# A cached-attention decode kernel: the scheduling context's critical section spans the whole program instead of the first loads alone

## The chip, the cores and the metric

The kernel runs on one core of one Trainium2 chip. The metric is the device time of one execution in microseconds (us); the figure that is compared is the median of several executions. Five runs of the kernel before gave a median of 666.26 us, with a lowest of 666.04 and a highest of 666.57. Beside the times there is one profiled execution, which took 666.55 us.

The core has five engines that run their own instruction streams: PE (TensorE, matrix products), DVE (VectorE), ACT (ScalarE), POOL (GpSimd) and SP (SyncE). They are ordered only by semaphores. SP and ACT each issue DMAs on a queue of their own, and all DMAs run on the same 16 DMA engines.

## The reference

One decoding step of a pre-norm transformer block, for four sequences and one new position each. The attention reads a cache of 4096 positions for 32 heads of 128, so that the keys and the values are 134 MB each and nearly all of the input. Cut to what matters:

```python
# x: (4, 1, 640); k_cache, v_cache: (4, 32, 4096, 128); all bfloat16
def _A_ref(x, k_cache, v_cache, wq, wo):
    q = (x @ wq).reshape(4, 1, 32, 128).transpose(0, 2, 1, 3)
    scores = jnp.einsum("bhqd,bhkd->bhqk", q, k_cache) * 128 ** -0.5
    p = softmax(scores)
    o = jnp.einsum("bhqk,bhkd->bhqd", p, v_cache)
    return o.transpose(0, 2, 1, 3).reshape(4, 1, 4096) @ wo

def _B_ref(x, w1, b1, w2):                       # 640 -> 1728 -> 640
    h = x @ w1 + b1
    return (h * jnp.tanh(softplus(h))) @ w2

h = x + _A_ref(layernorm(x), k_cache, v_cache, wq, wo)
out = h + _B_ref(layernorm(h), w1, b1, w2)
```

## The kernel before

**Tiling.** The 32 heads are taken in four groups of eight, and each group is worked through for the four sequences: 16 steps `i`, with `hg, b = divmod(i, 4)`. In a step the keys of eight heads of one sequence lie in one SBUF slot, 128 partitions x 32768 bfloat16 (8.4 MB): 16 partitions for each head, 256 positions on each partition. The values lie in another slot in the same way. There are three such slots, A, B and C. Keys go to A, B, A, B (`KS`) and values to C, C, A, C (`VS`). DVE multiplies the keys in place by the query (`mult`, L503), PE adds groups of products by matmuls with the identity (`fold`, L705), DVE finishes the sums (`reduce`, L514), ACT takes the exponential, and PE multiplies by the values (`pv_mm`). The normalisation of a group of heads runs at the head of the next group's turn (`norm`, `heads`). PE's work for the four groups is one hardware loop of four turns (`Fori`, L917). After the last turn `pe_tail` does the output projection, the second layer norm and the dense block.

**Order and queues.** Nothing is left to a scheduler: each engine's program is written out by hand as a Python function (`sync_prog`, `pool_prog`, `act_prog`, `dve_prog`, `pe_prog`), and each is in the order in which it is issued. `Prog.do` emits an instruction and counts up a semaphore; `Prog.need` emits a wait for a count. The functions run twice: once dry, to note at which count each event happens, and once live. SP issues every large load: `wq` (5.2 MB, into slot C), the first two key blocks, then values and keys in turn as the slots come free, and at last the weights `wo`, `w1` and `w2`. ACT issues the small loads of `x` and of the bias `b1`. Each of them stores one half of the output (`store`, L248), on semaphores `OUT0` and `OUT1`.

**Head.** The program is built inside a tile context of the language. `first_loads` (L275) holds the loads of `wq`, `x`, key block 0 and key block 1. It is emitted alone inside a critical section of that context (L936 and L937), and then the context is closed (`tc.close()`, L939). The critical section and the closing emit instructions of their own, on the lines L936 and L939 of the profile: SP counts up a semaphore when its part of the section ends, the engines that took part answer by one each and SP waits for these answers; then come a barrier of all five engines, a clear of the context's own three semaphores by POOL, and a second such barrier. A barrier is a DRAIN on each engine that counts up one semaphore, a wait for the count of four by POOL, an increment by POOL of a release semaphore, and a wait for that on each of the other engines. Only after the second barrier do the five hand-written programs begin (L941 and L942). They allocate their semaphores straight from the core (`nc.alloc_semaphore`, L118), so that the context does not clear them.

**Tail.** After its half of the store, SP, and ACT after its half, calls `leave` (L254): it counts up `FIN`, waits until its own half has landed (`OUT0` or `OUT1` at 16) and takes the 16 off again. POOL, which has nothing to do by then, runs `clear` (L260): it waits for `FIN` at 2 and clears the other 24 semaphores in two ranges. Those instructions are on L257, L258, L262 and L263. After them each engine's program simply ends.

Of the kernel before, what the change touches and what calls it, by code (L numbers as in the profile page):

```python
# [72 lines left out]
def kernel(  # L73
# [13 lines left out]
    nc = tc.nc  # L87

    N, _, D = A_x.shape
    _, H, Sk, Dh = A_k_cache.shape  # L90
    F = B_w1.shape[1]
    P = 128
    DC = D // P
# [18 lines left out]
    SCALE = float(Dh) ** -0.5  # L112
    EPS = 1e-5

    book = Book()
    WSEM = ["WQ", "WT"] + [f"W{k}" for k in range(9)]
    for s in ["PE", "DV", "DVP", "DVA", "AC", "ACP", "PO", "KA", "KB", "VA", "VC", "X", "S", "OUT0", "OUT1", "FIN"] + WSEM:
        book.handles[s] = nc.alloc_semaphore(s)  # L118

    SB0, SLOT0 = 16512, 229344 - 3 * SLOT * 2  # L120
    at = [SB0]
# [1 line left out]
    def sb(name, shape, dt, region=at, top=SLOT0):  # L123
        size = 4 if dt == FP32 else 2
        for d in shape[1:]:
            size *= d
        size = -(-size // 32) * 32
        t = nc.alloc_sbuf_tensor_at(name, shape, dt, offset=region[0]).ap()
        region[0] += size
        assert region[0] <= top, (name, region[0])  # L130
        return t

    slot = {
        c: nc.alloc_sbuf_tensor_at(f"slot{c}", (P, SLOT), BF16, offset=SLOT0 + k * SLOT * 2).ap()
        for k, c in enumerate("ABC")
    }
# [28 lines left out]
    wq = slot["C"][:, 0 : DC * H * Dh].rearrange("p (c n) -> p c n", c=DC)  # L165
    x_bf = sb("x_bf", (N, D), BF16, setup, topC)
# [57 lines left out]
    x_rows = A_x.rearrange("b s d -> (b s) d")  # L224
# [5 lines left out]
    KS = {0: "A", 1: "B", 2: "A", 3: "B"}  # L230
    VS = {0: "C", 1: "C", 2: "A", 3: "C"}

    sp = Prog(nc.sync, book)
    po = Prog(nc.gpsimd, book)
    ac = Prog(nc.scalar, book)
# [3 lines left out]
    def tiles(src, i):  # L239
        hg, b = divmod(i, N)  # L240
        return src[b, hg * G : (hg + 1) * G].rearrange("h (q r) d -> (h q) (r d)", q=PG)

    def load(p, dst, src, key, sem):
        p.do(lambda: p.eng.dma_start(out=dst, in_=src), key, sem, 16)

    def store(p, h):
        c, n = CG // 2, D // 2
        p.need("o_bf")  # L248
        load(
            p, out_rows[:, h * n : (h + 1) * n].rearrange("b (k o) -> k b o", k=c),  # L250
            o_bf[h * P // 2 : (h + 1) * P // 2 : ROW, :], ("out", h), f"OUT{h}",
        )

    def leave(p, h):  # L254
        fin, o = book.handles["FIN"], book.handles[f"OUT{h}"]
        if p.live:
            p.eng.sem_inc(fin, 1)  # L257
            p.eng.wait_ge(o, 16).then_inc(o, -16)  # L258

    def clear():  # L260
        fin = book.handles["FIN"]
        nc.gpsimd.wait_ge(fin, 2).then_inc(fin, -2)  # L262
        nc.clear_and_free_semaphores(  # L263
            [h for k, h in book.handles.items() if k not in ("OUT0", "OUT1", "FIN")]
        )

    def k_load(i):
        c = KS[i % N]
        load(sp, slot[c][:, :], tiles(A_k_cache, i), ("K", i), "K" + c)

    def v_load(i):
        c = VS[i % N]
        load(sp, slot[c][:, :], tiles(A_v_cache, i), ("V", i), "V" + c)

    def first_loads():  # L275
        load(
            sp, slot["C"][:, 0 : DC * H * Dh], A_wq.rearrange("(p c) n -> p (c n)", c=DC), "wq", "WQ"
        )
        load(ac, x_bf[:, :], x_rows[:, :], "x", "X")
        k_load(0)  # L280
        k_load(1)

    def sync_prog():
        for hg in range(NHG):
            i = hg * N
            if hg:
                sp.need(("PV", i - 2))
                k_load(i)
                sp.need(("F", i - 1, NS - 1))
                k_load(i + 1)  # L290
            sp.need(("PV", i - 1) if hg else ("qb", NHG - 1))
            v_load(i)
            sp.need(("F", i, NS - 1))
            k_load(i + 2)
            sp.need(("PV", i))
            v_load(i + 1)
            sp.need(("F", i + 1, NS - 1))
            k_load(i + 3)
            sp.need(("F", i + 2, NS - 1))
            v_load(i + 2)  # L300
            sp.need(("PV", i + 1))
            v_load(i + 3)
        sp.need(("F", NT - 1, NS - 1))
        for q in range(NHG):
            load(
                sp, wo_sb[:, q, :, :],
                A_wo[q * QN : (q + 1) * QN, :].rearrange("(p j) n -> p j n", j=G), ("wo", q), f"W{q}",
            )
        w1_v = B_w1.rearrange("(p c) n -> p c n", c=DC)
        for k, (c0, c1) in enumerate(zip(W1S, W1S[1:])):  # L310
            load(sp, w1_sb[:, c0:c1, :], w1_v[:, c0:c1, :], ("w1", c0), f"W{NHG + k}")
        sp.need(("PV", NT - 2))
        load(sp, w2_tail[0:FT, :], B_w2[FM * P : F, :], "w2t", "WT")
        w2_v = B_w2[0 : FM * P, :].rearrange("(p j) n -> p j n", j=FM)
        for k, (j0, j1) in enumerate(zip(W2S, W2S[1:])):
            load(sp, w2_sb[:, j0:j1, :], w2_v[:, j0:j1, :], ("w2", j0), f"W{NHG + 2 + k}")
        store(sp, 0)
        leave(sp, 0)

    def pool_prog():  # L320
        g = nc.gpsimd
# [19 lines left out]

    def act_prog():
        a = nc.scalar
        ac.need("b1z")
        load(ac, b1T[:, 0:FM], B_b1[0 : FM * P].rearrange("(p j) -> p j", j=FM), "b1a", "S")
        load(ac, b1T[0:FT, FM : FM + 1], B_b1[FM * P : F].rearrange("(p o) -> p o", o=1), "b1b", "S")
        ac.need("eps", "mv")
        ac.do(
            lambda: a.activation(
                out=std[:, :], in_=mv[:, 1:2], func=ACT.Sqrt, bias=eps[0:N, :], scale=1.0  # L350
            ),
            "std", "AC",
        )
        for h in range(2):
            ac.need(("q", h))
            ac.do(
                lambda: a.copy(out=q_all[:, h * 512 : (h + 1) * 512], in_=red[:, h, :]),
                ("qa", h), "ACP",
            )
        for hg in range(NHG):  # L360
            ac.need(("qb", hg))
            ac.do(
                lambda: a.copy(
                    out=q_bc[:, hg, :, :].rearrange("p b d -> p (b d)"), in_=red[:, (2 + hg) % 4, :]
                ),
                ("qc", hg), "AC",
            )

        ac.need("ident")
        ac.do(  # L370
            lambda: a.copy(
                out=pv_sb[:, :, :], in_=ident[:, :].unsqueeze(1).to_broadcast([P, RQ, Dh])
            ),
            ("pvc", -1), "ACP",
        )

        def exp(i, s):
            b = i % N
            sl = slice(s * RS, (s + 1) * RS)
            ac.need(("R", i, s))  # L380
            ac.do(
                lambda: a.activation(  # L382
                    out=ex[:, sl], in_=s_f[:, sl], func=ACT.Exp, scale=SCALE,
                    accum_out=rs[:, b, s : s + 1],
                ),
                ("exp", i, s), "AC",
            )

        def copy(i):
            ac.need(("PV", i))  # L390
            ac.do(
                lambda: a.copy(  # L392
                    out=pv_sb[:, :, :].rearrange("p r d -> p (r d)"), in_=pv[:, :]
                ),
                ("pvc", i), "ACP",
            )

        for i in range(NT):
            b = i % N
            if i and b == 0:  # L400
                copy(i - 1)
            for s in range(NS):
                exp(i, s)
                if (b, s) in ((1, 1), (2, 2), (3, 2)):
                    copy(i - 1)
        copy(NT - 1)
        ac.need("var")
        ac.do(
            lambda: a.activation(
                out=std2[:, :], in_=var[:, :], func=ACT.Sqrt, bias=eps[:, :], scale=1.0  # L410
            ),
            "std2", "AC",
        )
        ac.need("h1")
        ac.do(
            lambda: a.activation(out=ta[:, :, :], in_=h1[:, :, :], func=ACT.Exp, scale=1.0),  # L416
            "ta", "AC",
        )
        store(ac, 1)
        leave(ac, 1)  # L420

    def dve_prog():
        v = nc.vector
# [485 lines left out]
    def pe_prog(live):  # L909
# [16 lines left out]

    progs = (
        (sp, sync_prog), (po, pool_prog), (ac, act_prog), (dv, dve_prog), (pe, lambda: pe_prog(pe.live))
    )
    first_loads()  # L930
    for p, f in progs:
        f()
    book.ready = True
    for p, f in progs:
        p.restart(True)
    with tc.tile_critical(name="k", no_gpsimd_drain=True):  # L936
        first_loads()  # L937
    tc.close()
    tc.compile()  # L939
    for p, f in progs:  # L940
        f()  # L941
        if p is po:  # L942
            clear()


# [28 lines left out]
```

The softmax here doesn't subtract the row's maximum and nothing guards it: scores larger than these inputs give would overflow.

## Time and profile before

| what | value |
|---|---|
| median of 5 runs | 666.26 us (666.04 to 666.57) |
| the profiled execution, its own time | 666.55 us |
| its span, first to last instruction | 665.1 us |
| what lies around the span | 1.45 us |
| bytes read from HBM | 283.35 MB, 426 GB/s over the span |
| DMA queue of SP, share of 16 engines | 98.9% |
| busy DVE, PE, ACT, POOL | 407.3, 399.3, 41.6, 3.3 us |

In the page's strip of 40 slices a digit is the busy share of a slice in tenths. In a timeline each line has the start, the time taken, the engine, the line of the kernel, the operation, what is written and what is read; `q` after an engine's name stands for its instruction queue, where DMAs are issued and semaphores are waited for. A question about one line of the kernel answers with the operations on it, how often each ran, the shortest, the median and the longest duration in ns, and the first and the last start in us. The wait of an instruction is not part of its duration: its start is the moment when its wait ended.

### The profile page before, as it was taken

What the parts mean: (1) busy time and instruction counts of PE and PEld (TensorE: products, weight loads), DVE (VectorE), ACT (ScalarE), POOL (GpSimd) and SP (SyncE); (2) the same over time, 40 slices, a digit from 0 to 9 for tenths busy, and PEclk for the clock granted to TensorE, in tenths of its full rate; (3) what the DMA queues carried; (4) which work ended last, traced back from release to release, by engine and by line L of the source; (5) the groups of instructions that cost most, each with busy time, mean ns of one, the idle gap of its engine ahead of it and who ended that gap; (6) DMA issues with size and microseconds to landing.
All of it is one profiled execution on the core that took longest, in us unless ns stands there. A gap on an engine that the chain in (4) does not pass through costs nothing. (4 is left out here: it accounts for less than half of the span.)

```text
span 665.1 us, 5193 instructions
## 1 busy us (share of the span) xinstructions
PE 399.3 (60%) x2747; PEld 80.2 (12%) x1787; DVE 407.3 (61%) x252; ACT 41.6 (6%) x158; POOL 3.3 (0%) x15
## 2 busy tenths in 40 slices
PE   0856658668317595848408395838335666755767
PEld 0600000101101010101100010100010001010147
DVE  1077988486048778677218798759207688948602
ACT  0200000000000000000000000000000000000011
POOL 1000000000000000000000000000000000000000
PEclk9768787968659796868658887879776769887865
DMA  9999999999999999999999999999999999999996
GB/s 379 439 438 441 415 414 441 439 434 439 431 438 426 426 441 422 441 434 441 438 418 434 441 422 441 434 438 442 410 441 434 426 441 438 438 430 422 438 401 250
DMA packets 6390, 283.50 MB, mean 426 GB/s; under 512 B 936, under 2 KB 1004, under 8 KB 1516
## 3 DMA queue, kind: packets, MB, share of 16 engines
q1 hardware_dynamic: 6138, 283.35, 98.9%
q8 instruction: 7, 0.11, 0.1%
q10 hardware_dynamic: 242, 0.01, 0.0%
q14 instruction: 3, 0.02, 0.0%
HBM read 283.35 MB, written 0.01 MB: 426 GB/s over the span
## 5 line engine op out<-in xcount | busy, mean ns | idle before, releaser
L503 DVE TENSOR_TENSOR slotA<-slotA,q_bc 128x8192 bf16<-128x8192 bf16 x32 | 140.7, 4416 | 106.3 <-DMA slotA<-in_A_k_cache_dram 106.3
L503 DVE TENSOR_TENSOR slotB<-slotB,q_bc 128x8192 bf16<-128x8192 bf16 x32 | 140.7, 4418 | 15.9 <-DMA slotB<-in_A_k_cache_dram 15.9
L514 DVE TENSOR_REDUCE s_f<-red 128x64 f32<-128x1024 f32 x64 | 78.0, 1219 | 101.7 <-PE red L705 101.6
L705 PE MATMUL red<-slotA,ident 128*128 128x512 bf16 x480 | 138.2, 452 | 0.0
L705 PE MATMUL red<-slotB,ident 128*128 128x512 bf16 x480 | 129.6, 430 | 0.0
L695 PE MATMUL red<-slotA,ident 128*128 128x512 bf16 x32 | 14.2, 445 | 120.1 <-PEq L49 120.1
L695 PE MATMUL pv<-slotC,e 128*32 128x512 bf16 x768 | 52.7, 436 | 37.9 <-PEq L49 37.9
L695 PE MATMUL red<-slotB,ident 128*128 128x512 bf16 x32 | 14.2, 443 | 86.6 <-PEq L49 86.6
L382 ACT ACTIVATE ex<-s_f 128x64 bf16<-128x64 f32 x64 | 16.4, 256 | 505.9 <-DVE s_f L514 505.9
L528 DVE TENSOR_TENSOR e<-ex,hmask 128x512 bf16<-128x512 bf16 x64 | 39.8, 684 | 0.0
L695 PEld LDWEIGHTS pv<-slotC,e 128*32 128x32 bf16 x768 | 22.7, 108 | 96.6 <-issue 83.2
L695 PEld LDWEIGHTS red<-slotA,ident 128*128 128x128 bf16 x32 | 3.2, 99 | 189.1 <-issue 189.0
L695 PEld LDWEIGHTS red<-slotB,ident 128*128 128x128 bf16 x32 | 3.2, 99 | 170.9 <-issue 170.9
L695 PEld LDWEIGHTS o_ps<-pv_sb,selo 128*32 128x32 f32 x136 | 13.5, 109 | 64.0 <-issue 63.9
L695 PE MATMUL o_ps<-pv_sb,selo 128*32 128x128 f32 x136 | 18.0, 276 | 0.0
L695 PE MATMUL pv<-slotA,e 128*32 128x512 bf16 x256 | 14.5, 380 | 0.6 <-PEq L49 0.6
L392 ACT COPY pv_sb<-pv 128x512 f32<-128x512 f32 x16 | 9.4, 586 | 72.3 <-PE pv L695 72.3
L382 ACT ACTIVATION_READ_ACCUMULATOR ex<-s_f 128x1 f32 x64 | 11.9, 186 | 0.0
L695 PE MATMUL red<-q_all,sel 32*128 32x128 bf16 x128 | 10.0, 269 | 0.8 <-PEq L49 0.8
L695 PEld LDWEIGHTS red<-q_all,sel 32*128 32x128 bf16 x128 | 9.8, 122 | 1.7 <-issue 1.7
L695 PEld LDWEIGHTS pv<-slotA,e 128*32 128x32 bf16 x256 | 6.7, 97 | 25.3 <-issue 19.5
L553 DVE RECIPROCAL rl<-misc 32x1 f32<-32x1 f32 x4 | 0.6, 150 | 14.8 <-PE misc L695 14.8
(95 smaller groups left out, 78.0 us busy)
## 6 DMA issues: line engine op xcount, KB each, us to landing
slotC<-in_A_wq_dram SPq DMA_DIRECT2D x1, 5120.0 KB, 15.5
slotB<-in_A_wo_dram SPq DMA_DIRECT2D x4, 1280.0 KB, 16.8
slotB<-in_B_w_dram SPq DMA_DIRECT2D x1, 1296.0 KB, 23.5
slotA<-in_B_w_dram SPq DMA_DIRECT2D x1, 960.0 KB, 27.3
slotB<-in_B_w_dram SPq DMA_DIRECT2D x1, 864.0 KB, 25.8
slotA<-in_B_w_dram SPq DMA_DIRECT2D x1, 800.0 KB, 28.7
slotA<-in_B_w_dram SPq DMA_DIRECT2D x1, 320.0 KB, 29.0
slotC<-in_A_v_cache_dram SPq DMA_DIRECT2D x12, 45.1
```

What stands on the lines that cost most here:

```text
L382: lambda: a.activation(out=ex[:, sl], in_=s_f[:, sl], func=ACT.Exp, scale=SCALE, accum_out=rs[:, b, s : s + 1],),
L392: lambda: a.copy(out=pv_sb[:, :, :].rearrange("p r d -> p (r d)"), in_=pv[:, :]),
L503: lambda: v.tensor_tensor(out=t, in0=t, in1=q_bc[:, hg, b, :].unsqueeze(1).to_broadcast([P, RS, Dh]), op=ALU.mult,),
L514: lambda: v.tensor_reduce(out=s_f[:, s * RS : (s + 1) * RS], in_=red[:, k : k + 2, :].rearrange("p k (r c) -> p (k r) c", c=CW), axis=AX.X ...
L528: lambda: v.tensor_tensor(out=e[:, sl, :], in0=ex[:, sl].unsqueeze(2).to_broadcast([P, RS, G]), in1=hmask[:, :].unsqueeze(1).to_broadcast( ...
L553: dv.do(lambda: v.reciprocal(out=rl[:, :], in_=l_ps), ("rl", hg), DV)
L695: lambda: nc.tensor.matmul(out_, lhsT=lhsT, rhs=rhs, start=start, stop=stop, skip_group_check=skip),
L705: return t.add_instruction(mybir.InstMatmult(name=nc.get_next_instruction_name(), engine=mybir.EngineType.PE, ins=[t.lower_ap(rhs), t.lowe ...
```

## The change

The critical section is entered at the top of the kernel function and is left when the function returns, so that all five programs stand inside it. The closing of the context, with its answers, barriers and clear, comes behind everything else. The semaphores are allocated from the context, which clears them there; `FIN`, `leave` and `clear` go away. The first loads are at the head of `sync_prog` and `act_prog`. At its end SP waits for both halves of the output; ACT waits for neither.

In the built programs the instructions between the first loads and the output stores are the same, in the same order on each engine, with the same waits, in both kernels. What stands elsewhere is this:

- Ahead of the programs: PE, DVE and POOL wait by a branch for the section to open, as SP and ACT do in both kernels. The three steps that stood between the first loads and the programs (answers, first barrier, clear, second barrier) are gone from there.
- Behind the programs, on SP: a wait for `OUT1`, a branch that waits for `OUT0`, the count-up that ends the section, SP's own answer, two waits and a NOP that waits, for the answers of all five engines, and the two barriers.
- Behind the programs, on ACT, PE, DVE and POOL: the answer (which waits for SP's count-up) and the two barriers.
- Between the two barriers POOL clears one range of 32 semaphores: the 26 of the kernel and six of the context.

```diff
+    ctx.enter_context(tc.tile_critical(name="k", no_gpsimd_drain=True))
+
     book = Book()
     WSEM = ["WQ", "WT"] + [f"W{k}" for k in range(9)]
-    for s in ["PE", "DV", "DVP", "DVA", "AC", "ACP", "PO", "KA", "KB", "VA", "VC", "X", "S", "OUT0", "OUT1", "FIN"] + WSEM:
-        book.handles[s] = nc.alloc_semaphore(s)
+    for s in ["PE", "DV", "DVP", "DVA", "AC", "ACP", "PO", "KA", "KB", "VA", "VC", "X", "S", "OUT0", "OUT1"] + WSEM:
+        book.handles[s] = tc.alloc_semaphore(s)
...
-    def leave(p, h):
-        fin, o = book.handles["FIN"], book.handles[f"OUT{h}"]
-        if p.live:
-            p.eng.sem_inc(fin, 1)
-            p.eng.wait_ge(o, 16).then_inc(o, -16)
-
-    def clear():
-        fin = book.handles["FIN"]
-        nc.gpsimd.wait_ge(fin, 2).then_inc(fin, -2)
-        nc.clear_and_free_semaphores(
-            [h for k, h in book.handles.items() if k not in ("OUT0", "OUT1", "FIN")]
-        )
...
-    def first_loads():
-        load(
-            sp, slot["C"][:, 0 : DC * H * Dh], A_wq.rearrange("(p c) n -> p (c n)", c=DC), "wq", "WQ"
-        )
-        load(ac, x_bf[:, :], x_rows[:, :], "x", "X")
-        k_load(0)
-        k_load(1)
+    def sync_prog():
+        load(sp, slot["C"][:, 0 : DC * H * Dh], A_wq.rearrange("(p c) n -> p (c n)", c=DC), "wq", "WQ")
...
         for hg in range(NHG):
             i = hg * N
             if hg:
                 sp.need(("PV", i - 2))
-                k_load(i)
+            k_load(i)
+            if hg:
                 sp.need(("F", i - 1, NS - 1))
-                k_load(i + 1)
+            k_load(i + 1)
...
         store(sp, 0)
-        leave(sp, 0)
+        sp.need(("out", 0), ("out", 1))
...
     def act_prog():
         a = nc.scalar
+        load(ac, x_bf[:, :], x_rows[:, :], "x", "X")
...
         store(ac, 1)
-        leave(ac, 1)
...
-    first_loads()
     for p, f in progs:
         f()
     book.ready = True
     for p, f in progs:
         p.restart(True)
-    with tc.tile_critical(name="k", no_gpsimd_drain=True):
-        first_loads()
-    tc.close()
-    tc.compile()
-    for p, f in progs:
         f()
-        if p is po:
-            clear()
```

More of the change, by code (lines that the diff above doesn't have):

```diff
@@ L252, in store, with k_load, v_load @@
         )
-    def leave(p, h):
-        fin, o = book.handles["FIN"], book.handles[f"OUT{h}"]
-        if p.live:
-            p.eng.sem_inc(fin, 1)
-            p.eng.wait_ge(o, 16).then_inc(o, -16)
-    def clear():
-        fin = book.handles["FIN"]
-        nc.gpsimd.wait_ge(fin, 2).then_inc(fin, -2)
-        nc.clear_and_free_semaphores(
-            [h for k, h in book.handles.items() if k not in ("OUT0", "OUT1", "FIN")]
-        )
[L267 to L273, printed above, removed]
-    def first_loads():
-        load(
-            sp, slot["C"][:, 0 : DC * H * Dh], A_wq.rearrange("(p c) n -> p (c n)", c=DC), "wq", "WQ"
-        )
-        load(ac, x_bf[:, :], x_rows[:, :], "x", "X")
-        k_load(0)
-        k_load(1)
-    def sync_prog():
+    def sync_prog():
+        load(sp, slot["C"][:, 0 : DC * H * Dh], A_wq.rearrange("(p c) n -> p (c n)", c=DC), "wq", "WQ")
+        def k_load(i):
+            s = KS[i % N]
+            load(sp, slot[s][:, :], tiles(A_k_cache, i), ("K", i), "K" + s)
+        def v_load(i):
+            s = VS[i % N]
+            load(sp, slot[s][:, :], tiles(A_v_cache, i), ("V", i), "V" + s)
         for hg in range(NHG):
```

## The prediction

> **What bounds the kernel now.** I read the page's strip and its DMA queues first, then the timeline of the first 17 us and of the last 3 us, and last the single lines on which the context's own instructions stand. The strip and the queues say what the 665.1 us are made of:
>
> ```profile
> DMA  9999999999999999999999999999999999999996
> GB/s 379 439 438 441 415 414 441 439 434 439 431 438 426 426 441 422 441 434 441 438 418 434 441 422 441 434 438 442 410 441 434 426 441 438 438 430 422 438 401 250
> q1 hardware_dynamic: 6138, 283.35, 98.9%
> HBM read 283.35 MB, written 0.01 MB: 426 GB/s over the span
> ```
>
> The 16 DMA engines are busy in every slice, and only the last falls off. So 283 MB of cache and weights bound the kernel, and an edit can act in two places: ahead of the first load or behind the last one. The change lies in just these two places, so the timeline is read there. This is the head:
>
> ```profile
> 0.97 0.38 SPq L244 DMA_DIRECT2D slotC<-in_A_wq_dram  x1
> ...
> 1.87 0.43 SPq L244 DMA_DIRECT2D slotB<-in_A_k_cache_dram  x1
> 3.37 0.20 POOL L322 MEMSET ident<- 128x128 bf16 x1 [2.93 <-POOLq L939]
> 3.44 0.06 DVE L425 MEMSET eps<- 128x1 f32 x1 [3.44 <-PEq L939]
> ...
> 4.18 1.00 ACTq L244 DMA_DIRECT2D b1T<-in_B_b_dram  x2
> ...
> 8.18 0.09 DVE L495 MEMSET rsm<- 128x32 f32 x1
> ...
> 16.61 4.46 PE L695 MATMUL red<-slotC,lnT 128*32 128x512 bf16 x40 [8.06 <-PEq L49]
> ```
>
> SP has issued its three loads by 2.30 (1.87 + 0.43). Between that and 3.37, the first instruction of a program, nothing is computed: this is where the context is closed. Then the layer norm of `x` and the masks are made, done by 8.3. And then PE waits until 16.6 for `wq`, the first transfer on the queue. The closing of the context lies beside that transfer.
>
> The instructions of the closing, found by their lines (the first four rows) and, for comparison, the branch that closes PE's loop:
>
> ```profile
> L936 SPq EVENT_SEMAPHORE  x2: 17/17/17, 2.3 to 2.5; - x2
> L939 SPq COMPARE_BRANCH  x1: 33/33/33, 0.8 to 0.8; - x1
> L939 PEldq EVENT_SEMAPHORE  x2: 51/51/51, 2.9 to 3.3; - x2
> L939 POOLq EVENT_SEMAPHORE_RANGE_CLEAR  x1: 51/51/51, 3.0 to 3.0; - x1
> L917 PEldq COMPARE_BRANCH  x4: 76/213/239, 176.4 to 641.2; - x4
> ```
>
> And the tail, with the waits for the output and the two clears:
>
> ```profile
> 662.71 0.33 DVE L691 CAST o_bf<-red 128x160 bf16<-128x160 f32 x1 [2.29 <-PE red L695]
> 663.06 0.66 SPq L244 DMA_DIRECT2D out_dram<-o_bf  x1
> 663.07 0.64 ACTq L244 DMA_DIRECT2D out_dram<-o_bf  x1
> L263 POOLq EVENT_SEMAPHORE_RANGE_CLEAR  x2: 91/100/109, 664.0 to 664.2; - x2
> L258 SPq EVENT_SEMAPHORE  x1: 17/17/17, 664.8 to 664.8; - x1
> L258 ACTq EVENT_SEMAPHORE  x1: 17/17/17, 665.0 to 665.0; - x1
> ```
>
> POOL clears the semaphores while the output is still under way: the second clear starts at 664.2, and SP's half lands at 664.8, ACT's at 665.04. That wait of ACT is the last instruction of the span. Nothing stands behind it.
>
> **The head.** Removed between the first loads and the programs: about 1.1 us of closing; and the programs no longer wait for SP's three issues. PE, DVE and POOL start when the section opens, near 0.9 where ACT's first load stands, instead of at 3.4. So layer norm and masks are ready up to 2.5 us sooner, about 5.8 instead of 8.3. I take 0 for this: PE still waits for `wq` until 16.6, and the cover of 8 us becomes one of 10.8. The loads of `wq`, `x` and the two key blocks keep their place and their order on SP and ACT, with the same branch ahead of them, so the stream starts at 0.97 as before. The two loads of `b1` on ACT's queue come at about 1.8 instead of 4.18. If both issues (1.00 us together) held up SP's third load, it would go out 1 us later; it is behind `wq` and key block 0, of which DVE waits for the second until 36.8, so this costs 0. Their bytes (3.3 KB) travel beside `wq` in both kernels. Were all cover lost, the head would be worth 2.5 us to the good; the rivals take this up.
>
> **The body.** Same instructions, same order, same waits on SP's queue: 0, with an uncertainty of the spread of the five runs, 0.3 us to either side.
>
> **The tail, what goes.** `leave` and `clear` cost nothing today: the increments of `FIN` and both clears lie between 663.7 and 664.3, beside the store that lands at 665.04. Taking them away gains 0. ACT's own wait goes too; SP now waits for `OUT1` as well, which comes at 665.04 as before, since ACT's issue is not moved.
>
> **The tail, what comes.** SP is the only one that waits; behind it all five engines stand at the section's end, and nothing of the closing can start before 665.04. The cover that the closing had (`wq`) is not there. Step by step:
>
> 1. From the wait for `OUT1` to the count-up that ends the section: a wait (on the next instruction after 0.06, as from SP's wait at 2.55 to its NOP at 2.61) and the branch that waits for `OUT0`. The branch at 0.81 was followed by SP's first load at 0.97, so 0.16. Together 0.22. Bounds: 0.12, if the branch costs no more than a wait, and 0.30, with PE's taken loop branch of 0.24.
> 2. From the count-up to the end of the second barrier: in the head this ran from 2.34 to 3.36 (PE's last wait starts at 3.31 and takes 0.05), so 1.01. Bounds 0.9 to 1.1 (2.30 to 3.44 is the longest reading, up to DVE's first instruction).
> 3. SP waits for five answers instead of two, with two waits and a NOP in place of one and a NOP: one step more, 0.06 (0 to 0.12).
> 4. POOL's clear: three semaphores took 51 ns, 11 took 91 and 13 took 109, which is 5 to 6 ns for each more (9 between the last two). For 32 that is about 210 ns, 0.16 more than what step 2 holds (0 to 0.26). It stands between the barriers, so all of it counts; a gain is excluded, as 32 are not fewer than three.
>
> The sum is 0.22 + 1.01 + 0.06 + 0.16 = 1.45, from 665.04; the span ended 0.02 behind that, so the span grows by 1.43, to 666.5. The low ends make 1.0, the high ends 1.8. With the 1.45 us around the span the profiled execution would take 667.98, against 666.55. The median of the five runs is 0.29 below that execution, so the forecast is 666.26 + 1.43 = 667.69, and 0.2% of the median is 1.33: about what a measurement of this kernel can tell from no change lies just below the sum.
>
> [...]
>
> **The rivals.**
>
> *It costs nothing that counts.* Either the closing runs partly beside the landing of the store, or it is shorter than in the head because four of five engines have long been idle. For it: ACT, PE, DVE and POOL have their branches behind them when SP comes. Against it: the answers wait for SP's count-up, and the barriers follow it. A closing of half the price gives +0.7, 667.0; none at all gives 666.3.
>
> *Faster, by the head.* If the chain of the whole kernel hung on the preparation of `x`, the 2.5 us would be earned and the tail paid: -2.5 + 1.43 = -1.1, or 665.2. It decides if the first projection (16.61) is released by `lnT` and not by `wq`, that is, if `wq` landed before about 8.3. For it speaks only the idle stretch of all programs up to 3.4. Against it stands PE's idle time of 8.06 us ahead of that matmul, with `lnT` long done, and a DMA share of 9 tenths throughout.
>
> *Dearer: something waits once more at the end.* [...] The instruction queue's row says seven packets and 0.1% of 16 engines' span: 0.001 x 16 x 665.1 / 7 = 1.5 us each (0.8 to 2.3, as the share is rounded). Or the end of the program, part of the 1.45 us around the span, grows because all five engines now end together, where PE, DVE and POOL were done 0.7 us or more before ACT. Either gives +1 to +1.5 more: 668.7 to 669.2. For it: no trace here shows this code behind the programs. [...]
>
> *It does not do what it says.* The loop of the four groups and the store by two queues, of which its name speaks, are in both programs; only the place of the closing differs. This is no separate case of time.
>
> **How the numbers follow.** The closing paid in full, 667.3 to 668.1 with 667.7 likeliest: 0.56, of which 0.40 lies above 667.59 (+0.2%) and 0.16 below. Dearer: 0.22. Cheaper by half or free: 0.18. Faster: 0.04. So faster 0.04, within 0.2% 0.34 (0.16 + 0.18), slower 0.62. The range of 8 in 10 goes from 667.0, the half-priced closing, to 669.0, inside the dearer case.
>
> **What would show it.** In the profile after: `wq` issued at 0.97 and the first projection at 16.6 though the first DVE instruction stands near 0.9; the waits for `OUT1` and `OUT0` at about 665.0; a range clear of about 210 ns near 666.2; the last wait of PE near 666.5; a span of 666.5. The prediction is wrong if the projection moves with the preparation, if the closing takes under 1.0 or over 1.8 us from the landing to the last wait, or if the time around the span is no longer 1.45 us.

## The result

The changed kernel takes 667.96 us (median of 22 runs, 667.52 to 668.51); the kernel before, measured again beside it, 666.40 us (42 runs, 665.77 to 667.07). The ratio is 1.0024 with a 95% interval of 1.0018 to 1.0030: slower by 1.56 us, or 0.24%. The profiled execution took 668.09 us, against 666.55.

### The profile after

First the page's strip, the large queue and the DMA total of the changed kernel:

```profile
span 666.3 us, 5193 instructions
DMA  9999999999999999999999999999999999999995
q1 hardware_dynamic: 6138, 283.35, 98.7%
```

The same packets, the same bytes, one digit lower in the last slice: the span is 1.2 us longer. Next its head, from the timeline:

```profile
0.95 0.20 POOL L306 MEMSET ident<- 128x128 bf16 x1 [0.51 <-SPq L115]
0.96 0.38 SPq L246 DMA_DIRECT2D slotC<-in_A_wq_dram  x1
1.02 0.06 DVE L409 MEMSET eps<- 128x1 f32 x1 [1.02 <-SPq L115]
...
1.76 1.49 ACTq L246 DMA_DIRECT2D b1T<-in_B_b_dram  x2
...
1.86 0.84 SPq L246 DMA_DIRECT2D slotB<-in_A_k_cache_dram  x1
...
2.98 0.87 DVE L413 BATCH_NORM_STATS2 stats<-x_bf 4x6 f32<-4x320 bf16 x2 [1.91 <-DMA x_bf<-in_A_x_dram]
...
6.51 0.18 PE L679 MATMUL y_ps<-xT,ident 128*128 128x20 bf16 x1 [0.45 <-PEq L49]
...
16.57 3.92 PE L679 MATMUL red<-slotC,lnT 128*32 128x512 bf16 x36 [9.88 <-PEq L49]
```

The first programs start 2.4 us sooner. By the matmul on `xT` only 1.86 of these are left (6.51 against 8.37), because DVE now has to wait for `x` until 2.98. And by the first projection nothing is left: 16.57 against 16.61, with PE idle for 9.88 us ahead of it instead of 8.06.

Then its tail, from the timeline and from the lines of the waits (L52, L246), of the section's end (L115) and of the closing (L945):

```profile
662.86 0.66 SPq L246 DMA_DIRECT2D out_dram<-o_bf  x1
662.87 0.64 ACTq L246 DMA_DIRECT2D out_dram<-o_bf  x1
L52 SPq EVENT_SEMAPHORE  x1: 17/17/17, 664.8 to 664.8; - x1
L246 SPq COMPARE_BRANCH  x1: 33/33/33, 664.9 to 664.9; - x1
L115 SPq EVENT_SEMAPHORE  x3: 17/28/28, 665.1 to 665.3; - x3
L945 POOLq EVENT_SEMAPHORE_RANGE_CLEAR  x1: 207/207/207, 665.8 to 665.8; - x1
L945 PEldq EVENT_SEMAPHORE  x2: 51/51/51, 665.7 to 666.2; - x2
```

ACT's half of the output lands at 664.83, 0.2 sooner than in the profile of before. From there the waiting instructions follow each other without a pause: the branch at 664.90, the count-up at 665.06, the clear at 665.80, PE's last wait at 666.25, which ends the span at 666.30. In the kernel before ACT's wait alone stood behind the landing. So the profiled 1.54 us are made of -0.21 (an earlier landing in this one execution), +1.45 (1.47 us from the landing to the end of the span, against 0.02) and +0.30 outside the span (668.09 - 666.30 = 1.79, against 666.55 - 665.06 = 1.49). The 1.45 that stands as "around the span" ahead of the prediction comes from the span rounded up to 665.1; by the end of ACT's wait, 665.04 + 0.02, it is 1.49.

### The profile page after: what moved, and what is told of

It is laid out like the page before. It is cut to its first block, busy times and chain, and to the rows that moved or that the text cites. A ratio compares the mean times of both kernels' runs of the same rounds, so it can differ in the third digit from the quotient of the medians.

```text
span 666.3 us, 5193 instructions
## 1 busy us (share of the span) xinstructions
PE 395.7 (59%) x2747; PEld 80.7 (12%) x1787; DVE 407.1 (61%) x252; ACT 41.5 (6%) x158; POOL 3.3 (0%) x15
## 5 line engine op out<-in xcount | busy, mean ns | idle before, releaser
L689 PE MATMUL red<-slotB,ident 128*128 128x512 bf16 x480 | 127.1, 424 | 0.0
L679 PE MATMUL red<-slotB,ident 128*128 128x512 bf16 x32 | 14.1, 441 | 87.7 <-PEq L49 87.7
L679 PEld LDWEIGHTS red<-q_all,sel 32*128 32x128 bf16 x128 | 10.3, 127 | 1.3 <-issue 1.3
L679 PE MATMUL red<-slotC,lnT 128*32 128x512 bf16 x40 | 4.1, 594 | 9.9 <-PEq L49 9.9
```

The lines of the kernel that those rows point to most:

```text
L679: lambda: nc.tensor.matmul(out_, lhsT=lhsT, rhs=rhs, start=start, stop=stop, skip_group_check=skip),
L689: return t.add_instruction(mybir.InstMatmult(name=nc.get_next_instruction_name(), engine=mybir.EngineType.PE, ins=[t.lower_ap(rhs), t.lowe ...
```

## The experiments

Three theories stood at the start. A: the closing costs its whole length because it lost its cover, and a second part of the loss lies outside the span, because engines that used to be done early now end late. B: the part outside the span belongs to the barriers and the clear, or is scatter. C: the loss is in the stream. All times are medians; "around" is the time of a run less its span, the median over the runs of a kernel. It scatters far less than the time. In the 92 runs of the kernel before that were made beside the experiments it is 1.52, in 84 of them between 1.45 and 1.59 (the span is given to 0.1 us) and in the other 8 up to 1.79, while the time moves by more than 1 us. The changed kernel has 1.80, most runs 1.75 to 1.82 and four between 2.03 and 2.08.

### The closing ahead of the first loads

```diff
     with tc.tile_critical(name="k", no_gpsimd_drain=True):
-        first_loads()
+        nc.sync.nop()
+        nc.scalar.nop()
     tc.close()
     tc.compile()
+    first_loads()
```

> The kernel before, with the critical section empty and the context closed ahead of the first loads instead of behind them; nothing else is changed. Theory A (the closing costs what it takes wherever no transfer lies over it): the section's end, two answers, two barriers and the clear of three semaphores, 1.0 to 1.1 us, come ahead of the load of wq, which goes out near 2.0 instead of 0.97; the whole stream follows, so +1.0 to +1.1 us in the span and in the time, 667.4, and the time around the span stays at 1.45. Theory C (the changed kernel loses in the stream or in the loop, and the closing is cheap): the stream is bound elsewhere and takes the late start up again, +0 to +0.3.

Measured: 667.39 us against 666.29 (ratio 1.0017, 1.0008 to 1.0026), around 1.51. The large loads, from SP's timeline of this kernel:

```profile
1.95 0.39 SPq L244 DMA_DIRECT2D slotC<-in_A_wq_dram  x1
2.40 0.41 SPq L244 DMA_DIRECT2D slotA<-in_A_k_cache_dram  x1
2.85 0.43 SPq L244 DMA_DIRECT2D slotB<-in_A_k_cache_dram  x1
```

All three go out 0.98 us later, and in this profile the store of the output is still 0.96 later (664.02 against 663.06). The time is 1.10 longer, by the interval 0.5 to 1.7: the closing, laid bare at the head, costs its length, and the stream does not make it good. The time around the span stays. Theory C is out for this place.

### All five engines end together

```diff
+    GO = ['GOPE', 'GODVE', 'GOPOOL']
...
             p.eng.wait_ge(o, 16).then_inc(o, -16)
+            if h == 1:
+                for g in GO:
+                    p.eng.sem_inc(book.handles[g], 1)
...
         if p is po:
             clear()
+    for g in GO:
+        eng = {"PE": nc.tensor, "DVE": nc.vector, "POOL": nc.gpsimd}[g[2:]]
+        eng.wait_ge(book.handles[g], 1).then_inc(book.handles[g], -1)
```

> The kernel before, with one more wait at the end of PE's, DVE's and POOL's programs for a count that ACT gives when its half of the output has landed, so that all five engines end together; no barrier and no clear is added. Theory A (the time around the span grew from 1.45 to 1.79 in the changed kernel because engines that used to be done early now end last): the span grows by 0.1 to 0.25 (three counts by ACT, one wait each), and the time around it goes to about 1.8; time +0.4 to +0.6, 666.9. Theory B (the growth around the span belongs to the barriers and the clear, or is scatter between executions): the time around stays at 1.45, time +0.1 to +0.25.

Measured: 667.04 against 666.29 (1.0011, 1.0002 to 1.0020), around 1.90. The profile shows ACT's half landing at 665.44 and the added waits right behind it, POOL's as the last:

```profile
L950 PEldq EVENT_SEMAPHORE  x1: 51/51/51, 665.6 to 665.6; - x1
L950 DVEq EVENT_SEMAPHORE  x1: 21/21/21, 665.6 to 665.6; - x1
L950 POOLq EVENT_SEMAPHORE  x1: 17/17/17, 665.7 to 665.7; - x1
```

There is no barrier and no clear behind the landing here, and yet the time around the span has grown by 0.38. Theory B falls; what follows ACT's landing inside the span grew from 0.02 to 0.27, which is three counts and a wait.

### One engine late at a time

The same edit with a list of one, for POOL, DVE and PE:

> The kernel before, POOL alone waiting for ACT's count at the end of its program. Theory A2 (each engine has an end of its own behind its last instruction, and the device time is the largest of last instruction plus end: SP 1.34 as in the merged wait, ACT 1.52 as in before, POOL 1.88 as read from the kernel after and from the run with all three late): POOL's wait stands 0.12 behind ACT's, the time around the span goes to 1.88, time +0.45 to +0.5, 666.8. A rival (it is PE or DVE whose end is dear, POOL only happened to be last): the time around the span stays at or under 1.52, time +0.1.

> The kernel before, DVE alone waiting for ACT's count at the end of its program. Theory A2 with POOL's end as the dear one: DVE's wait stands 0.12 behind ACT's, the time around the span is at most 1.82, the figure of the kernel after less what DVE ended before PE; time +0.0 to +0.35. The rival (DVE's end is the dear one): the time around the span 1.9, time +0.5.

> The kernel before, PE alone waiting for ACT's count at the end of its program. Theory A2 with POOL's end as the dear one: PE's wait stands 0.12 behind ACT's and takes 0.05, the time around the span is at most 1.79; time +0.0 to +0.4. The rival (PE's end is the dear one): the time around the span 1.8 to 2.0, time +0.5 or more.

With them belongs the merged tail wait alone, where SP is the last engine and ACT ends early:

```diff
     def leave(p, h):
-        fin, o = book.handles["FIN"], book.handles[f"OUT{h}"]
+        fin = book.handles["FIN"]
         if p.live:
             p.eng.sem_inc(fin, 1)
-            p.eng.wait_ge(o, 16).then_inc(o, -16)
+            if p is sp:
+                for o in (book.handles["OUT0"], book.handles["OUT1"]):
+                    p.eng.wait_ge(o, 16).then_inc(o, -16)
```

> The kernel before with the merged tail wait alone: SP waits for both halves of the output, one after the other, and ACT's program ends right after it has issued its half. Theory A: SP's second wait ends where ACT's did, at the landing of ACT's half, so span +0.0 to +0.05, time within 0.1 of before. A rival: the stretch around the span depends on ACT's end being late, and the time falls by 0.1 to 0.3.

| last engine | time | before beside it | ratio | around |
|---|---|---|---|---|
| SP (merged wait) | 666.24 | 666.29 | 1.0001 (0.9992 to 1.0010) | 1.34 |
| ACT (before) | | 666.29 | | 1.52 |
| DVE, 0.06 behind ACT | 666.47 | 666.46 | 1.0000 (0.9991 to 1.0009) | 1.46 |
| PE, 0.09 behind ACT | 666.53 | 666.46 | 1.0004 (0.9995 to 1.0013) | 1.65 |
| POOL, 0.05 behind ACT | 666.67 | 666.46 | 1.0003 (0.9994 to 1.0012) | 1.87 |

POOL's and ACT's last waits in the run with POOL late:

```profile
L259 ACTq EVENT_SEMAPHORE  x1: 17/17/17, 665.8 to 665.8; - x1
L950 POOLq EVENT_SEMAPHORE  x1: 17/17/17, 665.9 to 665.9; - x1
```

The times themselves decide nothing, their intervals all hold 1; POOL's median is 0.21 over before, where 0.45 to 0.5 were expected. The time around the span does decide. It fits this reading: what follows the last instruction depends on the engine, and the device time is the largest of "end of an engine's last instruction plus that engine's end". The absolute figures also hold whatever lies ahead of the first instruction; only their differences are shown. DVE's row fits ACT's end of 1.5 and so gives only an upper bound for DVE, 1.46. The dear one is POOL, at 1.87, as expected from the run with all three. The figures were then held against other kernels than those of the table: in the changed kernel POOL's last instruction ends 0.09 before the span does, so 1.87 - 0.09 = 1.78 (measured 1.80).

### The closing under the landing of the store

The kernel after, with SP's two waits behind the closing instead of ahead of it:

```diff
-    ctx.enter_context(tc.tile_critical(name="k", no_gpsimd_drain=True))
+    part = ctx.enter_context(ExitStack())
+    part.enter_context(tc.tile_critical(name="k", no_gpsimd_drain=True))
...
-        book.handles[s] = tc.alloc_semaphore(s)
+        book.handles[s] = (nc if s in ("OUT0", "OUT1") else tc).alloc_semaphore(s)
...
-        sp.need(("out", 0), ("out", 1))
...
         p.restart(True)
         f()
+    part.close()
+    tc.close()
+    tc.compile()
+    for o in (book.handles["OUT1"], book.handles["OUT0"]):
+        nc.sync.wait_ge(o, 16).then_inc(o, -16)
```

The two semaphores also moved to the front of the list, so that the clear stays one range.

> The kernel after, with the closing kept behind all programs but SP's waits for the two halves of the output moved behind the closing; the two semaphores are allocated from the core. So the closing runs beside the landing of the store, which is its cover. Theory A (the closing costs because nothing lies over it): it runs from 663.8 to about 665.0 counted in the times of before, the store lands at 665.04 as in before, the span is that of before to within 0.1; with POOL ending near 664.95 and an end of 1.88 the time is 666.6 to 666.8, +0.25 to +0.45 against before and 1.1 to 1.3 under the kernel after. Theory C (the changed kernel loses in the stream or by something else of the section): the time stays near 667.9.

Measured: 666.96 against 666.46 (1.0005, 0.9996 to 1.0014), around 1.71. The section's end stands on L116 of this kernel, the closing on L922, the waits for the output on L924:

```profile
662.56 0.66 SPq L247 DMA_DIRECT2D out_dram<-o_bf  x1
L116 ACTq DRAIN  x1: 665/665/665, 663.3 to 663.3; - x1
L116 SPq DRAIN  x1: 629/629/629, 663.4 to 663.4; - x1
L922 POOLq EVENT_SEMAPHORE_RANGE_CLEAR  x1: 201/201/201, 664.6 to 664.6; - x1
L924 SPq EVENT_SEMAPHORE  x2: 17/17/17, 665.1 to 665.2; - x2
```

+0.50 over before in place of +1.56: with the landing as its cover the same closing loses 1.06 of its price, and theory C is out for the tail too. The two intervals (0.9996 to 1.0014, and 1.0018 to 1.0030) do not touch, but they are wide: the 0.50 could be anything from nothing to 0.9. The profile gives a second figure: from ACT's landing, here estimated at 664.54 (start of ACT's issue plus the 1.97 of before), to the end of the execution it is 2.38, against 1.51 before (666.55 - 665.04) and 3.26 in the changed kernel (668.09 - 664.83). By that 0.88 of 1.75 were hidden. The median is just over the expected 0.25 to 0.45. The closing grew by 0.6, since ACT's and SP's DRAIN took 665 and 629 ns, where they took 8 and 13 in the changed kernel; so it ran to 665.13, past the landing. POOL's last instruction ends at 665.04, and 665.04 + 1.87 = 666.91, where the profiled execution took 666.92: what is left of the loss is that POOL, with the dearest end, now ends half a microsecond behind the landing.

### A smaller clear

The kernel after, with 24 of the 26 semaphores cleared by POOL while the store lands, as `clear` did before, which leaves the closing nine:

```diff
+    OWN = ["OUT0", "OUT1", "FIN"]
-        book.handles[s] = tc.alloc_semaphore(s)
+        book.handles[s] = (tc if s in OWN else nc).alloc_semaphore(s)
...
+    def clear():
+        nc.gpsimd.wait_ge(book.handles["FIN"], 2)
+        nc.clear_and_free_semaphores([h for k, h in book.handles.items() if k not in OWN])
```

SP and ACT count up `FIN` behind their stores, and `clear` stands behind POOL's program.

> The kernel after, with the clear cut: 24 of the 26 semaphores are allocated from the core and cleared by POOL under the landing of the store, as in before, so that the closing's own clear has 9 semaphores instead of 32. Theory A: the range clear in the closing takes about 80 ns instead of 207, the stretch from the landing to the last wait goes from 1.47 to 1.34, POOL's last instruction ends 0.13 sooner and the time falls by that, to 667.8. A rival (the closing's barriers wait for something else beside the clear): the stretch stays at 1.45 to 1.5.

Measured: 668.02 against 666.33 (1.0024, 1.0014 to 1.0033). The closing's own clear:

```profile
L956 POOLq EVENT_SEMAPHORE_RANGE_CLEAR  x1: 88/88/88, 665.2 to 665.2; - x1
```

From the landing (664.22) to the end of the span (665.54) it is 1.32 instead of 1.47: the clear's size is on the path, as expected. In the changed kernel and in the two runs with a late preparation this stretch is 1.47 each time, so the 0.15 is not the scatter of this stretch. The time does not show it, 0.15 us being less than medians of ten runs can tell here.

### The preparation later, by 10 and by 29 us

The kernel after, with 6 or 16 memsets of a scratch tile ahead of POOL's first instruction, of which the masks and the layer norm are waited for:

```diff
+        for n in range(6):
+            if n:
+                po.need(("late", n - 1))
+            po.do(lambda: g.memset(e[:, :, :], 0.0), ("late", n), "PO")
         po.do(lambda: g.memset(ident[:, :], 0.0), "id0", "PO")
```

> The kernel after, with six memsets of a scratch tile (128 x 2048 bfloat16) ahead of POOL's first one, each about 1.9 us by the rate of its memset of 960 elements, so that the masks, the layer norm and lnT come about 11 us later, near 17 instead of 7. Theory A (the head lies under the transfers): the first projection starts about 0.5 to 1.5 us later than 16.57 and the time does not change, 667.96 within 0.3. The rival (the chain of the kernel hangs on the preparation): +8 to +11 us.

> The same with sixteen memsets, about 30 us: lnT near 36, the queries on all partitions near 52 instead of 32, DVE's first product 15 us behind the landing of the first keys. Theory A, with the cover made of wq, both first key blocks and the first values: the third key block is asked for near 79 instead of 64, the first values have landed by 75, so the DMA queues stand empty for some 3 to 6 us, which a stream that bounds the kernel does not get back: +3 to +7. If the cover is larger than that: +0 to +1. If the preparation is on the chain: +20 or more.

With six: 668.06 against 666.33 (1.0023, 1.0014 to 1.0033), where the changed kernel has 667.96 against 666.40 (1.0024). From PE's timeline of this kernel:

```profile
17.00 0.18 PE L683 MATMUL y_ps<-xT,ident 128*128 128x20 bf16 x1 [0.45 <-PEq L49]
17.15 4.41 PE L683 MATMUL red<-slotC,lnT 128*32 128x512 bf16 x40
```

The preparation ends 10.5 us later and the first projection starts 0.6 later, now released by it and no longer by `wq`; the time stays. So the 2.4 us that the change gives back at the head are worth nothing, and a preparation 10 us later costs nothing, to within the half microsecond that the intervals leave.

This run and the one with the smaller clear also show what SP's long third load (0.84 in the changed kernel) has to do with ACT's issues of `b1`. First this run, then the smaller clear:

```profile
1.86 0.75 SPq L246 DMA_DIRECT2D slotB<-in_A_k_cache_dram  x1
12.81 0.99 ACTq L246 DMA_DIRECT2D b1T<-in_B_b_dram  x2
```

```profile
1.76 1.57 ACTq L247 DMA_DIRECT2D b1T<-in_B_b_dram  x2
1.86 0.43 SPq L247 DMA_DIRECT2D slotB<-in_A_k_cache_dram  x1
```

The load takes long with `b1` far away and short with `b1` beside it, so `b1` is not what lengthens it. It is the issue of `b1` that grows in the early place, from 1.00 to between 1.49 and 1.61 in all four profiles that have it there.

With sixteen: 678.28 us (1.0163, 1.0141 to 1.0185), 10.3 over the changed kernel, where 3 to 7 were expected. These are four runs, and one of them took only 675.12, which is 7.2 over. From the table by stretches of this kernel (start and end, length, busy time of PE, PE's weight loads, DVE, ACT, POOL, then PE's clock, the DMA share and GB/s):

```profile
60.00:70.00 10.00, 8.84 (x46) 1.20 (x12) 8.56 (x6) 0.70 (x4) 0.00 (x0) 0.98 1.00 433
70.00:80.00 10.00, 7.29 (x31) 0.66 (x9) 5.65 (x3) 0.35 (x2) 0.00 (x0) 0.83 0.27 118
80.00:90.00 10.00, 2.82 (x7) 0.10 (x1) 10.00 (x7) 0.35 (x2) 0.00 (x0) 0.72 1.05 419
```

Between 70 and 80 the DMA engines stand for 7.3 us: `wq`, the first two key blocks and the first values have come, and the third key block is asked for at 79.06 instead of 63.21 (this run, then the changed kernel):

```profile
79.06 0.33 SPq L246 DMA_DIRECT2D slotA<-in_A_k_cache_dram  x1
```

```profile
63.21 0.33 SPq L246 DMA_DIRECT2D slotA<-in_A_k_cache_dram  x1
```

That is the end of the cover, and the place is the expected one. The other 3 us, which one of the four runs does not have, are not explained, and no run looked into it.

### One store in place of two

```diff
     def store(p, h):
-        c, n = CG // 2, D // 2
         p.need("o_bf")
-        load(
-            p, out_rows[:, h * n : (h + 1) * n].rearrange("b (k o) -> k b o", k=c),
-            o_bf[h * P // 2 : (h + 1) * P // 2 : ROW, :], ("out", h), f"OUT{h}",
-        )
+        load(p, out_rows.rearrange("b (k o) -> k b o", k=CG), o_bf[0:P:ROW, :], ("out", h), f"OUT{h}")
...
-        store(ac, 1)
-        leave(ac, 1)
```

This is the kernel before with SP alone storing; POOL's `clear` waits for one count.

> The kernel before with one store of the whole output by SP in place of two halves by SP and ACT; POOL clears after one count. If the two issues held each other up (0.66 and 0.64 us in the profile of before, where SP's loads of the cache took 0.33 to 0.43): the issue takes about 0.4, the store lands 0.2 to 0.5 us sooner, and the time falls to about 665.9 to 666.1. If an issue of this pattern takes that long by itself, or 16 rows take longer to land than eight: within 0.2 us of before, or slower by up to 0.5.

> The single store by SP once more, as its first run left it open (666.08 against 666.29, ratio 0.9998 with 0.9989 to 1.0007). By the ends of the engines (SP's 1.34 instead of ACT's 1.5) and by a landing 0.2 sooner after the issue, the time should be 0.2 to 0.4 under before, 666.0; if the end of ACT was not what counted, within 0.1 of before.

Measured: 666.08 against 666.29 (0.9998, 0.9989 to 1.0007), and again 665.87 against 666.33 (0.9995, 0.9986 to 1.0004); around 1.35 and 1.37. The issue is not shorter when it is alone:

```profile
662.71 0.69 SPq L244 DMA_DIRECT2D out_dram<-o_bf  x1
```

so nothing speaks for the two issues of before having held each other up. It is not excluded: this store has 16 rows where each half has eight, and no run stored eight rows alone. The store lands 1.78 us behind the start of its issue, where ACT's half took 1.97. That and SP's shorter end, 0.19 + 0.17, would make it some 0.35 faster than the kernel before. An SP that ended even sooner would not help: in the first run's profile POOL's clear ends at 664.00 and SP's wait at 664.50, so 664.00 + 1.87 and 664.50 + 1.34 come to the same time within 0.03. Both medians lie lower, and both intervals hold 1. It stays a likely gain that is not shown.

## Why the prediction was right, point by point

The range (667.0 to 669.0) and the sign held, and 667.69 was 0.27 under the measured 667.96. Of this 0.14 is the kernel before itself, whose median is 666.40 in 42 runs and was 666.26 in the five shown. The forecast difference was 1.43, the measured 1.56. That the two lie so near is in part luck: the stretch around the span was 0.28 larger than forecast, and 0.17 that is not accounted for went the other way.

- **The head, 0.** Right in the time: first projection at 16.57, and the run with the preparation 10 us late shows the cover directly. Wrong in a detail: 1.9 us of the preparation were won and not 2.5, since the programs overtook the load of `x`. SP's third load did take longer, 0.84 against 0.43, but it went out at the same time, and the issues of `b1` are not the cause, as the run with the preparation 10 us late shows; what is stays open.
- **The body, 0 with 0.3 to either side.** The store was issued 0.2 sooner in the one profile (662.86 against 663.06), within that.
- **Step 1, landing to count-up, 0.22.** Measured 0.23. The branch was followed by the next instruction after 0.16, as in the head.
- **Steps 2, 3 and 4, 1.01 + 0.06 + 0.16 = 1.23.** Measured 1.24 from the count-up to the end of the span. The second wait came 0.06 behind the first, and the clear of 32 took 207 ns where about 210 were forecast. Only its place was misread: the head's clear starts 0.67 behind the count-up, so by the forecast's own steps it was due near 666.0 and not 666.2; it started 0.97 behind the landing.
- **"With the 1.45 us around the span".** This is the term that failed, and by its own last sentence ("or if the time around the span is no longer 1.45 us") the prediction was wrong here. It was carried over as a constant and is 0.28 (medians) to 0.30 (profiles) larger after the change. The prediction had it in its third rival, as the end of the program that grows because all five engines end together, and priced it at 1 to 1.5 us; its size is a fifth to a third of that. And not their number counts but which engine is among them: POOL alone makes it 1.87. The 1.5 us that the same rival takes for one packet of the instruction queue no run shows as a wait at the end: after the change the stretch from the count-up to the end of the span took 1.24, against the 1.23 of steps 2 to 4, which hold no such wait.
- **The rivals.** "Costs nothing that counts" fell in every run in which the closing was bare; it needs cover, and the run that gave it the landing of the store got about 1 us back (1.06 by the medians, 0.88 by the profiles). "Faster, by the head" fell with the late preparation: its point of decision, that `wq` lands before `lnT` is done, was not enough to make it true, for with six memsets `lnT` did release the first projection and the time stayed. The cover does not end at `wq`; it ends where the DMA queues run empty, between 10.5 and 29 us of delay.

The parts add up to 1.45 + 0.28 = 1.73 against the measured 1.56. The remaining 0.17 was not pinned down; the start of the store moves by more than that between executions (from 662.45 to 663.84 in the profiles of the runs with PE and with POOL late, whose work up to the store is that of before).

## What to carry to other kernels

In this kernel a fixed sequence, the context's answers, barriers and clear, cost what it takes where nothing lay over it (1.10 us ahead of the first load; behind the last store 1.47 up to the end of the span), and nothing (beside `wq`) or about half (beside the landing of the store, where 0.88 of 1.75 were hidden) where it ran beside a transfer that is waited for anyway. In a kernel bound by its stream, look for such bare places at these two ends first. The sequence's price elsewhere in the same trace could be carried over step by step, here to within 0.02 us. Count to the end of the program and not to the end of the span: subtract the span from the time (1.52 us before, 1.80 after), and look which engine ends last.

## What the runs showed that was not expected

- The time around the span depends on which engine ends last: SP 1.34 us, ACT 1.5, PE 1.65, POOL 1.87, DVE at most 1.46. In 13 of the 14 profiled executions the device time is, to within 0.05, the largest over the engines of the last instruction's end plus the engine's figure; one alone, the single store's second profile, took 0.25 more, as about one in ten runs of the kernel before did by 0.13 to 0.27. Between SP and POOL that is a difference of 0.53 us; what an engine does in its stretch no run shows.
- A DRAIN right behind the issue of the output took 665 ns on ACT and 629 on SP, against 8 and 13 once the output had landed, and 55 on SP behind the load of a key block. Both ended at 663.98, before the output had landed (near 664.5, an estimate: the start of ACT's issue in that profile plus the 1.97 that it took in the profile of before), so it is not the landing that they wait for; what it is stays open.
- With the preparation 29 us late, 7.3 us of empty DMA queues became a loss of 10.3 in the median, and of 7.2 in one run of the four.
